# One more chunk in seven block products, its weight forms made earlier, and key transfers issued from GpSimd: a two-layer attention and feed-forward kernel on one Trainium2 core

## The chip, the core and the metric

The kernel runs on one core of one Trainium2 chip. The metric is the device time of one execution in microseconds (us). A core has five engines with an instruction queue each, worked off in the order in which the program lists it: PE (TensorE, matmul), DVE (VectorE), ACT (ScalarE), POOL (GpSimd) and SP (SyncE, which here only issues DMA transfers). ACT and POOL issue DMA transfers too. An engine whose next instruction waits for something holds up all that stands behind it in its own queue.

## The reference

x is 2048 tokens by 576 features, in float32. Two layers with the same weights run one after the other; a layer is an attention part and a feed-forward part.

```python
x = x + _A_ref(_layernorm(x), wqkv, wo)   # 32 heads of 18; token i sees i, i-2, i-4, ..., i-14
x = x + _B_ref(_layernorm(x), w1, w2)     # silu(x @ w1) @ w2, 576 -> 4608 -> 576
x = x + _A_ref(_layernorm(x), wqkv, wo)
x = x + _B_ref(_layernorm(x), w1, w2)
```

## The kernel before, in words

The tokens are cut into four chunks of 512, so two layers make eight stages, s = 0 to 7 (s = 0 to 3 are the first layer's chunks, 4 to 7 the second's). Stage s has a front (`front(s)`, L1208: layer norm, attention, output projection, second layer norm) and a feed-forward part. While PE works on the feed-forward part of stage s, DVE and ACT work on the front of stage s + 1. Float32 products are made of float16 halves: a matmul row is split into a high and a low half, and the products high by high, high by low and low by high are summed.

**The feed-forward part in its plain form** (`ffn`, L1110) is used for s = 0 to 3. For each of 36 blocks of 128 hidden features PE runs 14 matmuls of 128x512 (L1137), ACT applies silu and makes the high half, DVE makes the low half (L1144). After each group of nine blocks the second product follows: 216 matmuls of 128x288 (L1156), whose sums DVE adds to x (`add_to`, L823).

**The form with seven block products** (`ffn_pairs`, L1022) is used for s = 4 to 7. A pair of hidden blocks, the two halves of the 576 input features and the two halves of the chunk make a two by two block product, which is computed with seven products for eight. Each of the seven takes 7 matmuls of 128x256 (L1041), so a pair takes 49. ACT copies a product out of PSUM and applies silu (L1045, L1064 to L1068), DVE adds products up (L1048), and both make the halves of the result (L1071, L1074). The second product is that of the plain form (L1095). This form needs two things that the plain one does not:

- seven combinations of the weights of each of 18 pairs. `prepare(q)` (L927) makes them once: POOL loads the raw weights (L936, L939), DVE forms sums (L947), ACT and DVE make high and low halves (L955, L962) in one buffer `wg`, and POOL stores them to DRAM as `wfs` (L967). Later SP loads them for each stage (L972).
- seven combinations of the normalised tokens. `forms` (L979) takes the place of `layer_norm` there: DVE makes differences (L993, L998), ACT and DVE make the halves (L1007, L1012, L1013), and SP transposes them into `xb` (L1017).

**The attention of one chunk** (`attention`, L677) runs over four units of 144 features. In the first layer the units of s = 1 to 3 are fetched from DRAM (`kv<-kd`, L689). In the second layer PE computes them (L646, 4 tasks of 14 matmuls for each unit), ACT copies them out of PSUM into `kv` and `qt` (L713, L715), and four DMA transfers inside SBUF, `kv<-kv`, bring each partition the keys and values of the partitions ahead of it (`halo`, L720 to L726; these are the key transfers of this text). In the second layer's first block of tokens POOL then saves an edge to DRAM (L734). DVE multiplies, reduces and weighs (L744 to L785), with an exponential on ACT (L767). `project` (L792) splits the result into halves (L803, L421), SP transposes it and PE multiplies by `wo` (L816).

**Order.** The program calls `op(engine, duration, function, reads, writes, priority)` for each piece of work, and `Plan.order` (L111) then lists all pieces for each engine by a list scheduler: an engine takes, of its pieces that are ready by the planner's own durations, the one with the lowest priority number. Front work of stage s has priority s - 1.0, the DVE, ACT and SP work of its feed-forward part s - 0.5, its PE work s + 0.5. `PREP` is the priority of all 18 `prepare` calls; at 2.6 they come behind the front of stage 3 (2.0) and the DVE and ACT work of its feed-forward part (2.5), and ahead of the front of stage 4 (3.0). The layer norm of stage 4 waits for the last `wfs`. The order so made is fixed when the program is built.

Transfers issued from ACT and SP share eight completion counters (`DMAHW0` to `DMAHW7` in the built program), those from POOL have eight of their own (`DMASW0` to `DMASW7`). The counters are given out in the order of the whole program, and an issue waits until the transfer that had its counter before has landed.

Of the kernel before, what the change touches and what calls it, by code (L numbers as in the profile page):

```python
# [16 lines left out]
P = 128  # L17
# [7 lines left out]
NC = 4  # L25
# [3 lines left out]
UC = D // NU  # L29
# [11 lines left out]
LNX = 512.0  # L41
G2 = (5, 4, 5, 4)
W2N = 11
PREP = 2.6


class Buf:
# [204 lines left out]
def sliding_attention_silu_ffn(ctx: ExitStack, tc: tile.TileContext, x, wqkv, wo, w1, w2, out):  # L252
    nc = tc.nc
# [5 lines left out]
    op = S.op  # L259

    def fl(t):
        return t.rearrange("p a b -> p (a b)")
# [5 lines left out]
    def T(b):  # L268
        return S.tags[b.tag][b.slot]
# [91 lines left out]
    def rows(t, row, dims):  # L361
        return bass.AP(tensor=t.tensor, offset=t.offset + row * t.shape[-1], ap=dims)
# [280 lines left out]
    def qkv_matmul(xT, w, j, m):  # L643
        pl = list(passes(lambda k: T(xT)[:, k, j * P:(j + 1) * P], w))
        for n, (a, b) in enumerate(pl):
            nc.tensor.matmul(T(m)[:, :3 * UC], a, b, start=n == 0, stop=n == len(pl) - 1)  # L646
# [30 lines left out]
    def attention(s, xT, wq, more=None):  # L677
        lay, c = divmod(s, NC)
        blk, par = divmod(c, 2)
        pr_ = s - 1.0  # L680
        o = Buf("o")
        for u in range(NU):
            kv, qt = Buf("kv"), Buf("qt")
            own = [(kv, j) for j in range(NJ)]
            if wq is None:
                def fetch(kv=kv, qt=qt, u=u):
                    row = blk * TB
                    q = nc.sync if s == 1 else nc.gpsimd
                    q.dma_start(T(kv).rearrange("p a b c -> p (a b c)"),  # L689
                                rows(kd[par][u], row, [[NJ * 2 * UC, P], [1, NI * 2 * UC]]))  # L690
                    q.dma_start(fl(T(qt)), rows(qd[par][u], row, [[NJ * UC, P], [1, NJ * UC]]))
                op("SP" if s == 1 else "POOL", 1.2, fetch, [("qd", c, u), ("qd0", u) if blk == 0 else ("eds", lay, par, u)],
                   own + [(qt, j) for j in range(NJ)] + [(kv, "halo"), (kv, "edge")], pr_, nbytes=P * 4 * UC * 26)
            else:
                w = wq(u)
                if blk == 0:
                    def clear(kv=kv):
                        nc.gpsimd.memset(T(kv)[0:2, 0:3], 0.0)
                        nc.gpsimd.memset(T(kv)[0:1, 3:7], 0.0)
                    op("POOL", 1.6, clear, [], [(kv, "edge")], pr_)  # L700
                else:
                    def edge(kv=kv, u=u):
                        a, b = T(kv)[0:2, 0:3], T(kv)[0:1, 3:7]
                        e = eds[lay, par, u]
                        nc.sync.dma_start(a.rearrange("p a b c -> p (a b c)"), e[:, 2 * UC:])
                        nc.sync.dma_start(b.rearrange("p a b c -> p (a b c)"), e[1:2, :])
                    op("SP", 0.8, edge, [("eds", lay, par, u)], [(kv, "edge")], pr_, nbytes=20000)
                for j in range(NJ):
                    m = Buf("zq" if lay else "misc")

                    def evac(j=j, m=m, u=u, kv=kv, qt=qt):
                        d = du[:, u:u + 1]
                        nc.scalar.activation(T(kv)[:, j + W - 1].rearrange("p a b -> p (a b)"), T(m)[:, UC:3 * UC],  # L713
                                             AF.Copy, scale=d)
                        nc.scalar.activation(T(qt)[:, j, :], T(m)[:, 0:UC], AF.Copy, scale=d)  # L715
                    op("PE", 2.7 if s else 2.9, lambda j=j, m=m, w=w: qkv_matmul(xT, w, j, m),
                       [(xT, j)] + w.keys, [m, (kv, "hold")] if lay else [m], pr_)
                    op("ACT", 0.9, evac, [m, ("su", u)], [(kv, j), (qt, j)], pr_ - (0 if s else 9))

                def halo(kv=kv):  # L720
                    t = T(kv)

                    for p0, n, i, m in ((0, 112, 3, 4), (112, 15, 3, 4), (0, 112, 0, 3), (112, 14, 0, 3)):
                        d = 1 if i else 2
                        nc.scalar.dma_start(t[p0 + d:p0 + d + n, i:i + m], t[p0:p0 + n, 11 - m:11])
                op("ACT", 3.2, halo, own, [(kv, "halo")], pr_ - 0.2, nbytes=P * 14 * UC * 4)  # L726
                if blk == 0:
                    def save(kv=kv, u=u):
                        t = T(kv)[P - 2:P, 7:11]
                        if lay == 0:  # L730
                            nc.gpsimd.dma_start(rows(kd[par][u], W - 1 + TB - 8, [[NJ * 2 * UC, 2], [1, NJ * 2 * UC]]),
                                                t.rearrange("p a b c -> p (a b c)"))
                        else:
                            nc.gpsimd.dma_start(eds[lay, par, u], t.rearrange("p a b c -> p (a b c)"))  # L734
                    op("POOL", 0.6, save, own, [("eds", lay, par, u)], pr_, nbytes=20000)
                if more:
                    more(u, w)
# [468 lines left out]
    X, XT, ahead = {}, {}, []  # L1206

    def front(s):  # L1208
        X[s] = load_x(s, s - 1.0 if s else -20)
        if s == 0:  # L1210
            no_keys()
            xT = layer_norm(X[0], -20, "xa", 3, PE_LN[0])
            x1 = layer_norm(load_x(1, -8.5, gate[0:1]), -8.5, "xb", False, PE_LN[1])
            x2 = layer_norm(load_x(2, -2.0, gate[3:4]), -2.0, "xb", True, PE_LN[2])

            def more(u, w):
                qkv_ahead(1, u, x1, w)
                qkv_ahead(2, u, x2, w)
                ahead.append((u, w))
            o = attention(0, xT, raw_wq, more)  # L1220
            x3 = layer_norm(load_x(3, -1.2, gate[11:12]), -1.2, "xa", True, PE_LN[3])
            for u in (2, 0, 1, 3):
                store_wq(u, ahead[u][1], PACE_WQ[u])
            for u in (0, 1, 3, 2):
                qkv_ahead(3, u, x3, ahead[u][1] if u != 2 else load_wq(2, -0.95))
            raw_wo()
        elif s < NC:
            o = attention(s, None, None)
        else:
            o = attention(s, layer_norm(X[s], s - 1.0, "xa", False, late=[("wfs", NP - 1)]), lambda u: load_wq(u, s - 1.0, "wz"))  # L1230
        project(s, o, X[s])
        XT[s] = layer_norm(X[s], s - 1.0, "xb", s == 1, s == 0) if s < NC else forms(X[s], s - 1.0)

    front(0)
    for s in range(NL * NC):

        (ffn if s < NC else ffn_pairs)(s, XT[s], X[s])
        if s == 0:
            for q in range(NP):
                prepare(q, PREP)  # L1240
        if s + 1 < NL * NC:
            front(s + 1)
# [29 lines left out]
```

## Time and profile before

| | us |
|---|---|
| median of 3 runs (lowest, highest) | 2207.78 (2200.92, 2210.1) |
| the profiled execution | 2208.64 |
| its span, first to last instruction | 2206.6 |
| busy: PE, DVE, ACT, POOL | 2139.0, 1578.4, 905.3, 347.2 |

The profiled execution lies 0.9 us above the median, and 2.0 us of it lie around the span. Times below are those of the span, counted from its start. The profile is read from the engine that is busy almost all the time (PE) to the few places where it is not, and from there to what it waited for. PE's work falls into clear stages: the feed-forward parts of s = 1 to 7 begin at 482.9, 711.3, 939.6, 1208.8, 1473.8, 1733.3 and 1999.9 us.

### The profile page before, as it was taken

The page shows a single profiled execution, that of the slowest core. Times are in us where ns is not written, and L with a number is a line of the kernel's source. Part 1 is how long each engine was busy: PE and PEld are TensorE (multiplying, and loading weights), DVE is VectorE, ACT ScalarE, POOL GpSimd, SP SyncE. Part 2 cuts the span into 40 slices and gives each one's busy share as a digit, 9 for nine tenths or more (in the row PEclk, how much of TensorE's full clock was granted, in tenths as well). Part 3 has the DMA queues.
Part 4 walks back from the last instruction along what each step waited for, and adds up shares of the span by engine and source line. Part 5 has one row for each costly group of instructions (what it writes and reads, how often), then busy time and mean ns, then how long its engine had stood idle before and what let it go on. Part 6 is the DMA issues. An engine that isn't in the chain of part 4 may idle for free.

```text
span 2206.6 us, 39058 instructions
## 1 busy us (share of the span) xinstructions
PE 2139.0 (97%) x15406; PEld 1503.4 (68%) x15406; DVE 1578.4 (72%) x2453; ACT 905.3 (41%) x1617; POOL 347.2 (16%) x575
## 2 busy tenths in 40 slices
PE   5999999899999999999999989999999998999999
PEld 3556556556666666665667767887788866888887
DVE  7999889799999854454985479755897567963222
ACT  6455676553223333333232333253442424433232
POOL 2133455333012424410000000000000000000000
PEclk9999999999999999999999999999999999999999
DMA  5577576786656576667445765486665954566443
GB/s 154 167 206 254 191 235 221 193 269 221 180 169 224 180 200 214 215 227 194 140 137 125 203 204 172 123 222 158 205 181 151 241 165 128 169 159 192 141 145 107
DMA packets 301776, 407.20 MB, mean 185 GB/s; under 512 B 135432, under 2 KB 220276, under 8 KB 295320
## 3 DMA queue, kind: packets, MB, share of 16 engines
q1 hardware_dynamic: 261936, 270.35, 43.3%
q0 software_dynamic: 31360, 112.83, 15.6%
q10 hardware_dynamic: 8296, 21.52, 3.6%
q8 instruction: 120, 1.97, 0.4%
q14 instruction: 64, 0.52, 0.1%
HBM read 289.62 MB, written 67.68 MB: 162 GB/s over the span
## 4 chain that ended last, share of the span: by engine, by line
PE 90%; DMA 5%; DVE 2%; ACT 1%; issue 1%; ACTq 0%; POOL 0%; SPq 0%; DVEq 0%; POOLq 0%
PE acc L1095 19%; PE acc L1156 19%; PE z L1137 18%; PE misc L1041 8%; PE z L1041 8%; PE z L646 7%; PE misc L646 6%; PE acc L816 5%; DMA kv<-kv 1%; DMA yo<-yh 1%; DMA h<-in_A_wqkv_dram 1%; DMA w1s<-w 1%; DMA w<-in_B_w_dram 1%; DVE pr L777 0%; DMA wq<-wqs 0%
## 5 line engine op out<-in xcount | busy, mean ns | idle before, releaser
L1137 PE MATMUL z<-xb,w 128*128 128x512 f16 x2016 | 443.9, 380 | 12.4 <-ACT hs L1139 5.2
L1095 PE MATMUL acc<-w,h 128*128 128x288 f16 x3456 | 439.2, 286 | 0.6 <-DVE x L1104 0.6
L1156 PE MATMUL acc<-w,h 128*128 128x288 f16 x3456 | 428.6, 286 | 0.0
L1156 PEld LDWEIGHTS <-h 128*128 128x128 f16 x3456 | 338.0, 98 | 88.3
L1095 PEld LDWEIGHTS <-h 128*128 128x128 f16 x3456 | 338.0, 98 | 85.4 <-issue 0.8
L1041 PEld LDWEIGHTS <-w 128*128 128x128 f16 x3528 | 346.3, 98 | 62.6 <-issue 17.3
L1137 PEld LDWEIGHTS <-w 128*128 128x128 f16 x2016 | 197.0, 98 | 247.6 <-DVE w L892 8.2
L823 DVE SCALAR_TENSOR_TENSOR x<-acc,d,x 128x576 f32<-128x576 f32 x135 | 109.8, 814 | 202.7 <-PE acc L1095 131.3
L1041 PE MATMUL misc<-xb,w 128*128 128x256 f16 x1764 | 224.5, 274 | 8.5 <-ACT hs L1064 5.6
L1041 PE MATMUL z<-xb,w 128*128 128x256 f16 x1764 | 224.6, 274 | 7.5 <-ACT hs L1045 7.2
L1139 ACT ACTIVATE hs<-z,d 128x512 f32<-128x512 f32 x144 | 98.4, 683 | 298.1 <-PE z L1137 292.7
L646 PEld LDWEIGHTS <-xa 128*128 128x128 f16 x1344 | 131.7, 98 | 116.8 <-issue 5.2
L744 DVE TENSOR_TENSOR pr<-qt,kv 128x2304 f32<-128x2304 f32 x64 | 163.4, 2554 | 14.3 <-DMA kv<-kv 10.4
L1144 DVE SCALAR_TENSOR_TENSOR h<-hs,sh,h 128x512 f16<-128x512 f32 x144 | 106.3, 747 | 90.0 <-ACT h L1141 89.8
L777 DVE TENSOR_TENSOR pr<-kv,pe 128x1152 f32<-128x1152 f32 x128 | 169.8, 1352 | 1.0
L748 DVE TENSOR_REDUCE lg<-pr 128x128 f32<-128x2304 f32 x64 | 163.1, 2549 | 1.3
L784 DVE TENSOR_TENSOR pr<-pr 128x1152 f32<-128x1152 f32 (+1 forms) x128 | 135.2, 1056 | 3.4
L816 PE MATMUL acc<-wo,yo 128*128 128x288 f16 x896 | 117.1, 291 | 8.0 <-DMA yo<-yh 7.8
L646 PE MATMUL misc<-wq,xa 128*128 128x432 f16 x574 | 112.5, 352 | 3.4 <-ACT xa L436 2.5
L646 PE MATMUL z<-wq,xa 128*128 128x432 f16 x602 | 114.4, 346 | 1.1 <-ACT hs L659 0.6
L816 PEld LDWEIGHTS <-yo 128*128 128x128 f16 x896 | 88.7, 99 | 33.6 <-DMA yo<-yh 8.1
L1180 POOL DMA_DIRECT2D out_dram<-x x12 | 6.5, 544 | 647.9 <-DVE x L823 637.2
(186 smaller groups left out, 2226.8 us busy)
## 6 DMA issues: line engine op xcount, KB each, us to landing
w<-wfs SPq DMA_DIRECT2D x504, 160.0 KB, 3.2
w<-w2s SPq DMA_DIRECT2D x252, 288.0 KB, 4.7
w<-w1s SPq DMA_DIRECT2D x108, 320.0 KB, 4.8
wfs<-xa POOLq DMA_DIRECT2D x18, 1120.0 KB, 5.3
wq<-wqs SPq DMA_DIRECT2D x17, 1080.0 KB, 6.3
kv<-kd POOLq DMA_DIRECT2D x8, 1584.0 KB, 8.0
w1s<-w POOLq DMA_DIRECT2D x36, 320.0 KB, 4.4
w<-in_B_w_dram POOLq DMA_DIRECT2D x36, 288.0 KB, 4.2
```

The source lines that it names most:

```text
L646: nc.tensor.matmul(T(m)[:, :3 * UC], a, b, start=n == 0, stop=n == len(pl) - 1)
L744: nc.vector.tensor_tensor(T(pr), T(qt)[:, j:j + 2, None, :].to_broadcast([P, 2, W, UC]), win(T(kv), j, 2), op=ALU.mult)
L748: nc.vector.tensor_reduce(T(lg)[:, j:j + 2].rearrange("p a w h -> p (a w h)"), T(pr).rearrange("p a w (h d) -> p (a w h) d", d=DH), axis=A ...
L777: nc.vector.tensor_tensor(T(pr)[:, a].rearrange("p w (h d) -> p w h d", d=DH), v, T(pe)[:, j + a, :, :, None].to_broadcast([P, W, UH, DH]) ...
L784: nc.vector.tensor_tensor(t[:, :, 0:h, :], t[:, :, 0:h, :], t[:, :, h:2 * h, :], op=ALU.add)
L816: nc.tensor.matmul(T(acc)[:, h, 0:288], a, b[:, h * 288:(h + 1) * 288], start=n == 0, stop=n == len(pl) - 1)
L823: nc.vector.scalar_tensor_tensor(t, T(acc)[:, :, 0:288], d, t, op0=ALU.mult, op1=ALU.add)
L1041: nc.tensor.matmul(t, w[:, u, :], v[:, r, :], start=first and m == 0, stop=m == 6, skip_group_check=True)
L1095: nc.tensor.matmul(T(acc)[:, h, 0:288], T(hb[t])[:, a, f, j * P:(j + 1) * P], T(wbs[t][f])[:, w, h * 288:(h + 1) * 288], start=t == 0 and ...
L1137: nc.tensor.matmul(T(z), v, u, start=m == 0, stop=m == len(pl) - 1)
L1144: op("DVE", 0.75, lambda hs=hs, h=h, f=f: nc.vector.scalar_tensor_tensor(T(h)[:, 1, :], T(hs), shs[i][:, f:f + 1], T(h)[:, 0, :], op0=ALU. ...
L1156: nc.tensor.matmul(T(acc)[:, h, 0:288], T(hb[q])[:, a, j * P:(j + 1) * P], T(wbs[q][0])[:, w, h * 288:(h + 1) * 288], start=q == 0 and m = ...
```

## The change

A new constant `S2 = 3` stands where the number of chunks, 4, stood in two places: stage 3, the first layer's fourth chunk, now goes through `forms` and `ffn_pairs` in place of `layer_norm` and `ffn`. `PREP` goes from 2.6 to 1.6, so the 18 `prepare` calls come ahead of stage 3's front (2.0). In the second layer (`lay` is 1) the four key transfers of each unit are issued from POOL in place of ACT, and the planner counts 2.6 us of POOL for them in place of 3.2 us of ACT.

```diff
-PREP = 2.6
+PREP = 1.6
+S2 = 3
...
-                        nc.scalar.dma_start(t[p0 + d:p0 + d + n, i:i + m], t[p0:p0 + n, 11 - m:11])
-                op("ACT", 3.2, halo, own, [(kv, "halo")], pr_ - 0.2, nbytes=P * 14 * UC * 4)
+                        (nc.gpsimd if lay else nc.scalar).dma_start(t[p0 + d:p0 + d + n, i:i + m], t[p0:p0 + n, 11 - m:11])
+                op(*(("POOL", 2.6) if lay else ("ACT", 3.2)), halo, own, [(kv, "halo")], pr_ - 0.2, nbytes=P * 14 * UC * 4)
...
-        XT[s] = layer_norm(X[s], s - 1.0, "xb", s == 1, s == 0) if s < NC else forms(X[s], s - 1.0)
+        XT[s] = layer_norm(X[s], s - 1.0, "xb", s == 1, s == 0) if s < S2 else forms(X[s], s - 1.0)
...
-        (ffn if s < NC else ffn_pairs)(s, XT[s], X[s])
+        (ffn if s < S2 else ffn_pairs)(s, XT[s], X[s])
```

The new line moves every later line of the file down by one: L1041 of the kernel before is L1042 of the change.

The two orders are the same on every engine up to the front of stage 3. **First place: DVE, where they part.** DVE is at the projection of stage 2 (L803, L421) and the first multiplication of stage 3's attention (L744). Before:

```order
L803 TENSOR_SCALAR yh<-o,so 128x576
L421 SCALAR_TENSOR_TENSOR yh<-o,so,yh 128x512
L421 SCALAR_TENSOR_TENSOR yh<-o,so,yh 128x64
L744 TENSOR_TENSOR pr_89<-qt_84,kv_82 128x2304
L748 TENSOR_REDUCE lg_86<-pr_89 128x128
L823 SCALAR_TENSOR_TENSOR x_81<-acc_106,d_270,x_81 128x576
```

And of the change (`wq` and `xa` are where the raw and the prepared weights lie):

```order
L804 TENSOR_SCALAR yh<-o,so 128x576
L422 SCALAR_TENSOR_TENSOR yh<-o,so,yh 128x512
L422 SCALAR_TENSOR_TENSOR yh<-o,so,yh 128x64
L963 SCALAR_TENSOR_TENSOR xa<-wq,accw,xa 128x4x256
L963 SCALAR_TENSOR_TENSOR xa<-wq,accw,xa 128x4x128
L963 SCALAR_TENSOR_TENSOR xa<-wq,accw,xa 128x3x256
L963 SCALAR_TENSOR_TENSOR xa<-wq,accw,xa 128x3x128
L745 TENSOR_TENSOR pr_89<-qt_84,kv_82 128x2304
L824 SCALAR_TENSOR_TENSOR x_81<-acc_106,d_270,x_81 128x576
```

Four rows of `prepare` now stand ahead of the multiplication, and so it goes on: up to the projection of stage 3, twelve `prepare` calls have had their sums (L947) on DVE where before six had. On PE that projection moves with them: it stood behind the first 90 of the 216 matmuls of the second product of stage 2's first group, and stands behind the first 18 of the second group's.

PE has the same work ahead of stage 3's feed-forward part in both orders (its row 11298 is the first of that part in both); behind that row it has 36 x 14 matmuls of 128x512 (L1137) before and 18 x 49 of 128x256 (L1042) in the change.

**Second place: ACT, at the third unit of the attention of s = 7**, worked on during the feed-forward part of stage 6 (L713 and L715 copy out keys and queries, L1045 to L1066 belong to the feed-forward part). Before:

```order
L713 ACTIVATE kv_82<-misc_104,du 128x288
L715 ACTIVATE qt_84<-misc_104,du 128x144
L1045 ACTIVATE wq<-misc_103 128x256
L725 DMA kv_82<-kv_82 112x1152
L725 DMA kv_82<-kv_82 15x1152
L725 DMA kv_82<-kv_82 112x864
L725 DMA kv_82<-kv_82 14x864
L1045 ACTIVATE hs<-z_101 128x256
L1064 ACT_TABLE_LOAD
```

And of the change:

```order
L714 ACTIVATE kv_82<-misc_103,du 128x288
L716 ACTIVATE qt_84<-misc_103,du 128x144
L768 ACTIVATE pe_88<-lg_86 128x256
L1046 ACTIVATE wq<-z_101 128x256
L1046 ACTIVATE wq<-z_102 128x256 x2
L1046 ACTIVATE hs<-misc_103 128x256
```

The four issues are gone from between the copies. On POOL they stand between the write of stage 5's result and that of stage 6's (`out_dram`), where before these writes followed one another. **Third place: POOL, from the last write of stage 5's result on.** Before:

```order
L1180 DMA out_dram<-x_81 128x576
L1180 DMA out_dram<-x_74 128x576
L1180 DMA out_dram<-x_75 128x576
L1180 DMA out_dram<-x_76 128x576
L1180 DMA out_dram<-x_77 128x576
```

And of the change, the first two of the four units that stand between the two results:

```order
L1181 DMA out_dram<-x_81 128x576
L726 DMA kv_82<-kv_82 112x1152
L726 DMA kv_82<-kv_82 15x1152
L726 DMA kv_82<-kv_82 112x864
L726 DMA kv_82<-kv_82 14x864
L726 DMA kv_83<-kv_83 112x1152
```

Each unit's four transfers follow the one before's; no other kind of work stands between them there.

## The prediction

> **What bounds the kernel now.** I read the page first: busy times, slices, and the shares of the chain that ended last.
>
> ```profile
> PE 2139.0 (97%) x15406; PEld 1503.4 (68%) x15406; DVE 1578.4 (72%) x2453; ACT 905.3 (41%) x1617; POOL 347.2 (16%) x575
> PE   5999999899999999999999989999999998999999
> DVE  7999889799999854454985479755897567963222
> PE 90%; DMA 5%; DVE 2%; ACT 1%; issue 1%; ACTq 0%; POOL 0%; SPq 0%; DVEq 0%; POOLq 0%
> ```
>
> PE is the bound: past the first slice it is busy 90% or more, but for three slices with an 8. DVE is nearly full through 14 slices (to 772 us) and has room behind them. So a term counts if it shortens PE's work, ends a PE wait, or makes PE wait.
>
> Next, the stages: PE's windows from stage 1 on, one for each feed-forward part (length, then the busy time of PE, PEld, DVE, ACT, POOL, with counts).
>
> ```profile
> 482.90:711.20 228.30, 228.30 (x1482) 144.65 (x1480) 221.01 (x261) 80.77 (x106) 40.78 (x69) 1.00 0.65 205
> 711.20:939.60 228.40, 228.40 (x1482) 144.78 (x1481) 137.65 (x217) 83.70 (x115) 89.16 (x149) 1.00 0.67 208
> 939.60:1208.80 269.20, 269.20 (x1706) 166.66 (x1704) 185.05 (x273) 87.68 (x150) 20.54 (x31) 1.00 0.56 161
> 1208.80:1473.70 264.90, 259.03 (x2084) 204.31 (x2082) 186.59 (x291) 99.92 (x202) 8.02 (x12) 0.99 0.64 181
> 1473.70:1733.30 259.60, 256.93 (x2084) 203.56 (x2083) 185.70 (x289) 98.41 (x198) 2.16 (x4) 1.00 0.66 181
> 1733.30:1999.80 266.50, 259.05 (x2084) 204.14 (x2082) 183.18 (x280) 98.74 (x198) 2.16 (x4) 0.99 0.63 171
> ```
>
> In stages 1 to 3 PE never pauses. Stages 4 to 6 do the same work three times in 264.9, 259.6 and 266.5 us; what differs is idle time.
>
> **The change part by part.** *The products of stage 3.* The chain of waits, in order of time, has the unit costs (start, length, what):
>
> ```profile
> 738.62 11.03 PE acc L1156 x90
> 749.65 3.43 PE acc L816 x28
> 778.80 27.20 PE z L1137 x126
> 913.30 26.46 PE acc L1156 x216
> 1208.98 3.06 PE z L1041 x28
> 1295.33 2.56 PE misc L646 x14
> ```
>
> A plain stage has 36 x 14 = 504 matmuls of 128x512, 4 x 27.20 = 108.8 us. The seven-product form has 18 x 49 = 882 at 3.06 / 28 = 0.109 us, 96.4 us. The rest is common to both: 4 x 26.46 = 105.8 for the second product, 16 x 2.56 = 41.0 for keys, queries and values, 4 x 3.43 = 13.7 for the projection, 160.5 together. The plain stage comes out at 269.3, where the window shows 269.2, so such sums hold. The new stage 3 is 96.4 + 160.5 = 256.9: **-12.3 us**, if nothing stops PE.
>
> *The key transfers.* By the same sum stages 4 to 6 should take 3 x 256.9 = 770.7 us; the windows add up to 791.0. So 20.3 us are lost. The groups of 1209 to 2000 us show where (last figure: idle time ahead, and what ended it):
>
> ```profile
> L1041 PE MATMUL misc<-xb,w 128*128 128x256 f16 x1339 | 170.5, 275 | 8.5 <-ACT hs L1064 5.6 <-ACT wq L1045 2.7
> L1041 PE MATMUL z<-xb,w 128*128 128x256 f16 x1309 | 167.5, 274 | 7.5 <-ACT hs L1045 7.2
> ```
>
> 16.0 us of idle, in three stalls of 5.6, 2.7 and 7.2, each ended by ACT freeing a PSUM bank. The timeline shows what held ACT there:
>
> ```profile
> 1306.12 9.77 ACTq L725 DMA_DIRECT2D kv<-kv  x4
> 1315.93 0.47 ACT L1064 ACTIVATE hs<-misc,accw 128x256 f32<-128x256 f32 x1 [9.57 <-DMA kv<-kv]
> 1316.46 1.65 PE L1041 MATMUL misc<-xb,w 128*128 128x256 f16 x7 [5.61 <-ACT hs L1064]
> ...
> 1569.69 6.91 ACTq L725 DMA_DIRECT2D kv<-kv  x4
> 1577.08 0.93 PE L1041 MATMUL misc<-xb,w 128*128 128x256 f16 x7 [2.67 <-ACT wq L1045]
> ...
> 1824.38 10.55 ACTq L725 DMA_DIRECT2D kv<-kv  x4
> 1834.98 0.38 ACT L1045 ACTIVATE hs<-z 128x256 f32<-128x256 f32 x1 [10.28 <-DMA kv<-kv]
> 1835.41 1.65 PE L1041 MATMUL z<-xb,w 128*128 128x256 f16 x7 [7.18 <-ACT hs L1045]
> ```
>
> Each time it is the third unit's four transfers. The fourth issue waits for a completion counter whose last transfer is still under way (the third unit's own in stages 4 and 6, the weights `wq` in stage 5), and PSUM copies stand behind it. All transfers of this kind from 1200 us on:
>
> ```profile
> L725 ACTq DMA_DIRECT2D kv<-kv x48: 534/816/1148, 1261.8 to 1873.5; - x48
> DMA to landing us min/median/max: 6.9/8.1/9.3
> ```
>
> An issue itself takes 0.5 to 1.1 us; the 7 to 10 us are waits for a landing. On POOL none of it stands ahead of a PSUM copy, and POOL's own eight counters are never back at the first while a unit's four are given out. So the mechanism goes, in stage 3 too, where PE now uses the narrower products. Of the 20.3 I take all 16.0 of idle and half of the 4.3 by which the matmuls after the stalls are slow: **-18 us**; ends 0 and -20.3.
>
> What the transfers cost on POOL the trace shows only by its neighbours, the fetches of stages 1 to 3:
>
> ```profile
> L689 POOL DMA_DIRECT2D kv<-kd x8: 528/542/566, 347.0 to 667.6; - x8
> DMA to landing us min/median/max: 6.3/7.9/10.2
> ```
>
> A larger transfer issued from POOL takes 0.53 to 0.57 us to issue and 7.9 to land, against 8.1 for those on ACT. So keys arrive between 2 us sooner and 3 us later (6.3 - 8.1, 10.2 - 6.9); I take no change. It concerns DVE alone, which is idle 70 us and more in each of stages 4 to 6, and POOL, busy 2 to 8 us there. The Trainium skill speaks against this edit: in "SBUF — State Buffer", section "Summary: rules for kernel authors", it advises against a transfer issued from POOL beside DVE work, since DVE in a two-port mode keeps POOL from writing descriptors. The rows just quoted lie where DVE is 97% busy (its 221.01 of 228.30) and show no issue above 0.57 us, so the trace does not bear it out. A second page, "DMA: Bandwidth & Descriptors", section "Issuing engines are not separate DMA queues", says that another issuing engine only saves the time of issuing, "usually small"; by it this term would be near 0, and the 9.77 us row speaks against that too.
>
> *The weight forms ahead of stage 3's attention.* This adds no work, but it moves DVE work into its fullest stretch. Cost and places:
>
> ```profile
> L962 DVE SCALAR_TENSOR_TENSOR xa<-wq,accw,xa 128x1024 f16<-128x1024 f32 (+1 forms) x72 | 62.0, 912 | 3.0 <-ACT xa L955 3.0
> L947 DVE TENSOR_TENSOR wq<-wq 128x384 f32<-128x384 f32 x72 | 36.9, 554 | 0.9
> 586.15 2.55 DVE L744 TENSOR_TENSOR pr<-qt,kv 128x2304 f32<-128x2304 f32 x1
> 740.89 0.52 DVE L803 TENSOR_SCALAR yh<-o,so 128x576 f16<-128x576 f32 x1
> 784.37 3.40 DVE L962 SCALAR_TENSOR_TENSOR xa<-wq,accw,xa 128x1024 f16<-128x1024 f32 x4 [0.29 <-ACT xa L955]
> 981.82 3.41 DVE L962 SCALAR_TENSOR_TENSOR xa<-wq,accw,xa 128x1024 f16<-128x1024 f32 x4 [0.78 <-ACT xa L955]
> ```
>
> One call costs DVE (62.0 + 36.9) / 18 = 5.5 us. Six more stand ahead of the projection of stage 3: 33 us, at 97% busy 34, so DVE splits that result at 740.9 + 34 = 775, not 740.9. In the new order PE comes to it behind the rest of the first group and the whole first product of the second: the second product from 738.6 without the projection, 26.46, to 765.1, then 27.20, then 18 matmuls, 2.2, so at 794.5 where it was 749.65. Before, the lead was 749.65 - 740.9 = 8.8 us; now it is 19.5. So: **0**. The cover is gone if the calls themselves are slow. They follow one another through one buffer: making, storing, landing. Where nothing else filled DVE, ten such cycles ran from 784.37 to 981.82 (first and last of eleven splits), 19.7 us each. Nine calls' splits stand between 586 us, where the orders part, and the projection; eight cycles make 158 us, and there are 189. It would break above 189 / 8 = 23.6 us a cycle.
>
> *The token forms of stage 3* replace a layer norm. Their price before, for stage 4:
>
> ```profile
> 1185.10 1.07 DVE L993 TENSOR_SCALAR xa<-x,mv,nt 128x576 f32<-128x576 f32 x2
> 1213.02 2.54 SPq L1017 DMA_TRANSPOSE xb<-yh  x2
> ```
>
> The last differences stood 24 us ahead of the products (1208.98), the last transposes 4 us behind them, and PE did not wait. In the change DVE has the last differences behind its work on the last block of stage 2's first product, and PE leaves that block one second product, 26.46 us, ahead of stage 3: about the same lead. **0**; ends 0 and, if all of it came late, the 28 us from 1185.1 to 1213.0.
>
> **The sum.** 2208.64 - 12.3 - 18 = **2178 us** for the profiled execution; the median of the runs shown is 0.9 us lower, which I leave out.
>
> **The rivals.** *Only the products pay* (the waits move to another engine or another unit, or stage 3 gets a stall of its own). For it: in the change ACT has an exponential (L768) where the transfers stood, which waits for DVE; against it: of the 12 units of stages 4 to 6, nine had no stall with the same neighbours. Time: 2208.6 - 12.3 = 2196; with a stall in stage 3 like the average of the others (20.3 / 3 = 6.8), 2203.
>
> *Keys come late from POOL.* This is what the skill's rule would do. If each of a unit's four issues lasted as long as a DVE multiplication, 2.55 us and not 0.54, the keys would be 8 us late; only the first unit of a stage has no cover, so 4 x 8 = 32 us of DVE lateness, against 70 us of room in a stage. It gives 2178 to 2210. The L689 row speaks against it.
>
> *The weight forms hold up stage 3* (the other side). If a cycle takes 30 us, half as long again as that mean, DVE comes to the projection 8 x (30 - 23.6) = 51 us after 775. Of the lead of 19.5 us, 8.8 was enough before, so 10.7 is spare; PE waits 51 - 10.7 = 40 us, and the time is 2218; at 33 us a cycle it is 2242. It decides from 23.6 + 10.7 / 8 = 25 us a cycle. For it: POOL's queue now has key fetches of stage 3 (L689) among these loads and stores; against it: the mean of 19.7.
>
> *The change does not do what it says*: excluded by the order, which shows 882 matmuls of 128x256 in stage 3 and no key transfers on ACT in the second layer.
>
> **How the numbers follow.** Forecast 0.62 (2171 to 2187: half of the 20.3 recovered is 2186, all of it 2176, and one of the three runs before lies 7 us below their median). Only the products 0.21 (2188 to 2203). Late keys 0.07 (2180 to 2210). Weight forms 0.10 (2205 to 2242). The range 2171 to 2200 holds the first, most of the second and half of the third, somewhat over 8 in 10. Two kernels closer than 0.5%, 11 us, cannot be told apart here; against 2207.8 that bound is 2196.7. Faster: 0.62, 0.11 of the second, 0.04 of the third, 0.77. Same: 0.10, 0.03 and 0.02 of the last, 0.15. Slower: 0.08.
>
> **What would show it.** Products: the window of stage 3 is 257 us from an unchanged start at 939.6, its first product about 96 us by the chain. Key transfers: no idle above 1 us ahead of L1042, and windows of 257 in stages 4 to 6. Weight forms: no idle ahead of L817 in stage 2 and 18 stores finished by about 910. Token forms: no idle ahead of the first L1042. It is wrong if PE waits at the projection in stage 2, or if stalls of 5 us stay in stages 3 to 6 with ACT or DVE as their end.

## The result and the profile after

| | before | after |
|---|---|---|
| median (lowest, highest), us | 2207.65 (2200.92, 2210.1) | 2189.35 (2184.02, 2198.78) |
| profiled execution, us | 2208.64 | 2198.78 |
| from the begin of stage 1 to the end of the span, us | 1723.7 | 1705.3 |

The ratio is 0.9918, with an interval from 0.9891 to 0.9945: the change makes the kernel faster, by about 18 us, where 30 were forecast. The profiled execution is the slowest of the four of the change. It comes to stage 1 at 491.7 us, 8.8 later than that of before, although the instructions up to there and on to 586 us stand in the same order; such begins lie between 480.5 and 491.7 in the runs below. So traces are compared from the begin of stage 1 on (last row of the table): -18.4 us, which agrees with the medians. The forecast in the same measure is 1723.7 - 30.3 = 1693.4.

The page of the change, PE's slices and the shares of the chain:

```profile
PE 2132.9 (97%) x15784; PEld 1541.9 (70%) x15784; DVE 1598.0 (73%) x2513; ACT 927.2 (42%) x1697; POOL 380.9 (17%) x639
PE   5999999899999999999999999999999999999999
PE 87%; DMA 6%; DVE 4%; ACT 1%; issue 1%; POOL 0%; SPq 0%; ACTq 0%; DVEq 0%; POOLq 0%
```

Of PE's three slices with an 8 only the one in the head is left; the shares of the chain that fell to DMA and DVE have grown. The windows of stages 1 to 6:

```profile
491.70:720.50 228.80, 228.54 (x1483) 144.76 (x1481) 218.88 (x273) 86.56 (x115) 69.12 (x118) 1.00 0.73 229
720.50:948.80 228.30, 228.30 (x1482) 144.87 (x1480) 157.55 (x247) 93.02 (x142) 70.02 (x116) 1.00 0.68 211
948.80:1207.70 258.90, 257.25 (x2084) 203.58 (x2082) 184.91 (x287) 99.70 (x202) 20.22 (x32) 1.00 0.67 184
1207.70:1466.30 258.60, 257.57 (x2084) 203.63 (x2082) 188.06 (x297) 98.48 (x198) 16.45 (x28) 1.00 0.68 184
1466.30:1731.30 265.00, 260.17 (x2091) 205.00 (x2090) 185.99 (x286) 97.06 (x197) 10.70 (x20) 0.99 0.67 181
1731.30:1991.10 259.80, 257.69 (x2085) 203.59 (x2084) 183.13 (x280) 95.95 (x196) 10.70 (x20) 1.00 0.63 174
```

Stage 3 went from 269.2 to 258.9. Stages 4 to 6 went from 791.0 to 783.4, where 773 was forecast. What is left there is seen in the groups of 1206 to 1990 us:

```profile
L1042 PE MATMUL misc<-xb,w 128*128 128x256 f16 x1351 | 170.8, 274 | 3.4 <-DVE wq L1049 2.2 <-DMA w<-wfs 1.1
L1042 PE MATMUL z<-xb,w 128*128 128x256 f16 x1302 | 165.0, 273 | 4.4 <-DMA w<-wfs 3.3 <-DVE h L1075 0.6 <-DVE wq L1049 0.5
L745 DVE TENSOR_TENSOR pr<-qt,kv 128x2304 f32<-128x2304 f32 x24 | 61.3, 2555 | 18.1 <-DMA kv<-kv 17.5
```

No idle ends with ACT. PE now waits for weights to land (`w<-wfs`, 4.4 us) and for DVE, and DVE stands 17.5 us for keys, in three waits, each at the first unit of a stage; before it was 9.0 us in two. All key transfers of 1200 to 2000 us, issued and landed:

```profile
L726 POOL DMA_DIRECT2D kv<-kv x48: 515/541/563, 1258.1 to 1844.6; - x48
...
DMA to landing us min/median/max: 4.3/8.4/11.0
```

An issue takes 0.54 us in the middle, and they land in 8.4. The largest of PE's waits is again at the third unit, of stage 5. The timeline there:

```profile
1553.86 0.32 SPq L593 DMA_DIRECT2D wq<-wqs  x1
...
1554.59 1.05 SPq L834 DMA_DIRECT2D w<-w2s  x2
1554.66 2.11 POOL L726 DMA_DIRECT2D kv<-kv  x4 [24.28 <-ACT qt L716]
...
1556.09 15.41 SPq L973 DMA_DIRECT2D w<-wfs  x15
...
1567.25 0.94 PE L1042 MATMUL z<-xb,w 128*128 128x256 f16 x7 [2.75 <-DMA w<-wfs]
```

And the windows of 5 us around it (last three columns: granted clock, DMA share, GB/s):

```profile
1545.00:1550.00 5.00, 5.00 (x29) 2.65 (x28) 4.90 (x4) 1.54 (x4) 0.00 (x0) 1.00 0.44 149
1550.00:1555.00 5.00, 5.00 (x32) 3.03 (x31) 4.93 (x3) 1.54 (x4) 0.34 (x1) 1.00 0.13 17
1555.00:1560.00 5.00, 5.00 (x48) 4.47 (x46) 4.75 (x8) 1.65 (x5) 1.76 (x4) 1.00 0.86 286
1560.00:1565.00 5.00, 4.49 (x41) 3.74 (x39) 4.93 (x7) 3.94 (x7) 0.00 (x0) 1.00 1.05 267
1565.00:1570.00 5.00, 2.75 (x17) 2.12 (x18) 3.47 (x7) 2.18 (x5) 0.00 (x0) 0.81 1.06 324
```

The DMA engines are nearly idle, then full: the unit's weights (1080 KB) and the keys (997 KB) are issued within 3 us, fifteen loads of block weights (160 KB each) from 1556.09 to 1571.5, and PE runs out of block weights. In the window in which the wait ends the granted clock is 0.81, and of the matmuls behind it the next fourteen took 3.14 us, where fourteen take 1.69 a little later: a wait costs more than its own length.

### The profile page after: what moved, and what is told of

Read it like the earlier page. It is cut to its first block, busy times and chain, and to the rows that moved or that the text cites. A ratio compares the mean times of both kernels' runs of the same rounds, so it can differ in the third digit from the quotient of the medians.

```text
span 2197.0 us, 40182 instructions
## 1 busy us (share of the span) xinstructions
PE 2132.9 (97%) x15784; PEld 1541.9 (70%) x15784; DVE 1598.0 (73%) x2513; ACT 927.2 (42%) x1697; POOL 380.9 (17%) x639
## 4 chain that ended last, share of the span: by engine, by line
PE 87%; DMA 6%; DVE 4%; ACT 1%; issue 1%; POOL 0%; SPq 0%; ACTq 0%; DVEq 0%; POOLq 0%
PE acc L1096 24%; PE acc L1157 13%; PE z L1138 13%; PE z L1042 10%; PE misc L1042 10%; PE z L647 7%; PE misc L647 5%; PE acc L817 5%; DMA w<-wfs 2%; DMA yo<-yh 1%; DMA w<-in_B_w_dram 1%; DVE pr L778 1%; DMA h<-in_A_wqkv_dram 1%; DVE pr L785 1%; DVE yh L422 0%
## 5 line engine op out<-in xcount | busy, mean ns | idle before, releaser
L1042 PEld LDWEIGHTS <-w 128*128 128x128 f16 x4410 | 431.8, 98 | 67.9 <-DMA w<-wfs 8.2
L1138 PE MATMUL z<-xb,w 128*128 128x512 f16 x1512 | 336.9, 383 | 11.5 <-ACT hs L1140 4.2
L1042 PE MATMUL misc<-xb,w 128*128 128x256 f16 x2226 | 280.3, 273 | 3.9 <-DVE wq L1049 2.2
L1138 PEld LDWEIGHTS <-w 128*128 128x128 f16 x1512 | 148.8, 99 | 191.0 <-DVE w L893 7.5
L1042 PE MATMUL z<-xb,w 128*128 128x256 f16 x2184 | 276.2, 273 | 5.6 <-DMA w<-wfs 4.0
L745 DVE TENSOR_TENSOR pr<-qt,kv 128x2304 f32<-128x2304 f32 x64 | 163.4, 2553 | 20.7 <-DMA kv<-kv 19.5
L1140 ACT ACTIVATE hs<-z,d 128x512 f32<-128x512 f32 x108 | 73.7, 682 | 165.8 <-PE z L1138 162.3
L1075 DVE SCALAR_TENSOR_TENSOR h<-wq,sh,h 128x1024 f16<-128x1024 f32 x60 | 76.8, 1280 | 65.0 <-ACT h L1072 65.0
L1145 DVE SCALAR_TENSOR_TENSOR h<-hs,sh,h 128x512 f16<-128x512 f32 x108 | 79.5, 746 | 34.7 <-ACT h L1142 34.4
```

What stands on the lines that cost most here:

```text
L745: nc.vector.tensor_tensor(T(pr), T(qt)[:, j:j + 2, None, :].to_broadcast([P, 2, W, UC]), win(T(kv), j, 2), op=ALU.mult)
L1042: nc.tensor.matmul(t, w[:, u, :], v[:, r, :], start=first and m == 0, stop=m == 6, skip_group_check=True)
L1138: nc.tensor.matmul(T(z), v, u, start=m == 0, stop=m == len(pl) - 1)
L1145: op("DVE", 0.75, lambda hs=hs, h=h, f=f: nc.vector.scalar_tensor_tensor(T(h)[:, 1, :], T(hs), shs[i][:, f:f + 1], T(h)[:, 0, :], op0=ALU. ...
```

## The experiments

Two theories for the part of the 18 us forecast for the key transfers that was not got. **Theory DMA:** the third unit's burst fills the DMA engines, and PE waits for weights behind the keys' bytes. **Theory keys:** DVE's waits for the keys set back the work that empties PSUM for PE. All times are from the begin of stage 1 (b) as well as medians; before is 1723.7 by b. There is one trace of each kernel, so b has the spread of a single execution: the two traces of the change differ by 3.3 us (1705.3 and 1702.0).

| run | median, us | ratio to before (interval) | b, us |
|---|---|---|---|
| e1 the change again | 2189.8 | 0.9926 (0.9903 to 0.9948) | 1702.0 |
| e2 keys from POOL alone | 2204.13 | 0.9977 (0.9961 to 0.9992) | 1719.6 |
| e3 all but the keys | 2205.22 | 0.9981 (0.9961 to 1.0001) | 1713.7 |
| e4 early weight forms alone | 2219.31 | 1.0056 (1.0034 to 1.0077) | 1739.5 |
| e5 no key transfers | 2173.99 | 0.9859 (0.9829 to 0.9888) | 1692.7 |
| e6 later landing planned | 2190.43 | 0.992 (0.99 to 0.9939) | 1704.2 |
| e7 keys from SP | 2193.86 | 0.9939 (0.9917 to 0.9961) | 1708.5 |
| e8 two transfers a unit | 2188.49 | 0.991 (0.9891 to 0.993) | 1702.0 |
| e9 thin keys | 2177.09 | 0.9836 (0.9823 to 0.9848) | 1695.3 |
| e10 unit weights from POOL | 2197.86 | 0.9932 (0.9915 to 0.9949) | 1714.9 |
| e11 e10 and e8 together | 2202.26 | 0.9951 (0.9939 to 0.9963) | 1716.3 |
| e12 keys unread | 2176.56 | 0.9854 (0.9825 to 0.9883) | 1695.3 |

**e1, the change as it is.**

> The changed kernel once more, for its spread and a second trace. In its first trace PE lost 14.5 us in stages 3 to 6 (258.7, 258.7, 265.0, 259.7 us where the sum gives 256.9), in a 4.6 us wait for weights in stage 5 and some ten of 0.3 to 1.6 us; and stage 1 began at 491.7, 9 us later than in the kernel before, although the order is the same up to 586 us. If the 9 us are chance, stage 1 begins nearer to 483 now and the time is 2184 to 2190. If they belong to the change, the start stays at 490 or above. If the 4.6 us wait belongs to the order, it is in this trace too, at the third unit of stage 5.

The change repeats, and the late begin of stage 1 does not (486.2). Stages 3 to 6 took 259.2, 258.3, 261.8 and 260.2 us. Stages 4 to 6 add up to 780.3, 10.7 less than before. The longest wait for weights is at the third unit of stage 5 again, 2.3 us for 2.75 in the first trace (not the 4.6 that the expectation names), so it belongs to the order.

**e2, the key transfers from POOL alone.** `S2` and `PREP` as before (4 and 2.6).

> Only the key transfers go from POOL; stage 3 in its plain form, weight forms late. The prediction's term: -18 us, 2190, and no PE idle above 1 us ahead of L1041. If the traces of the two kernels add up (20.3 us lost in stages 4 to 6 before, 12.7 after): -7.6 us, 2200, with waits for weights and for DVE in place of those for ACT. If the change lives from its products alone: 2207.

It gained 4.1 us by b, 0.23% by the ratio. The groups of 1206 to 2000 us, where before had 16.0 us of idle ended by ACT:

```profile
L1041 PE MATMUL misc<-xb,w 128*128 128x256 f16 x1351 | 171.5, 273 | 6.4 <-DMA w<-wfs 4.6 <-DVE wq L1048 1.8
L1041 PE MATMUL z<-xb,w 128*128 128x256 f16 x1302 | 165.5, 273 | 6.2 <-DMA w<-wfs 2.8 <-ACT wq L1045 1.7 <-DVE wq L1048 1.6
```

The stalls behind ACT's issues went (1.7 us that end with ACT are left), and 7.4 us of waiting for weights came in their place. Stages 4 to 6 took 787.8 us for 791.0.

**e3, everything but the key transfers.** They stay on ACT:

```diff
-(nc.gpsimd if lay else nc.scalar).dma_start(
+nc.scalar.dma_start(
-op(*(("POOL", 2.6) if lay else ("ACT", 3.2)), halo,
+op("ACT", 3.2, halo,
```

> Seven products for stage 3 and the early weight forms, key transfers left on ACT. The products save 12.3 us. In this order the fourth transfer of the third unit has its own unit's counter again in stages 3 and 6, so if the counters make the stalls, there is one of 5 to 8 us in each of them (ACT held by kv<-kv) and none of that size from the unit's own counter elsewhere: 2195 to 2203. If the stalls came from something else and the products are all there is: 2189, as the whole change.

The products alone gained little, because a stall came to stage 3 that it had not had. The timeline of the third unit of stage 3:

```profile
1050.34 0.47 ACT L1065 ACTIVATE hs<-misc,accw 128x256 f32<-128x256 f32 x1 [10.47 <-DMA kv<-kv]
...
1050.86 1.65 PE L1042 MATMUL misc<-xb,w 128*128 128x256 f16 x7 [6.51 <-ACT hs L1065]
```

Stage 3 took 264.8 us for 258.9 in the change. With the transfers on POOL this stall is absent, so the products pay in full only with the other edit. The stalls came where the counters put them: 6.5 us in stage 3 and 6.4 in stage 6, and at most 2.65 in stages 4 and 5. That supports the account of completion counters. The gain is 10.0 us by b but 3.0 by the medians, with an interval that reaches 1, and the time lies above the 2195 to 2203 that were expected.

**e4, the early weight forms alone.** `PREP = 1.6`, nothing else.

> Only the priority of the weight forms, 1.6 for 2.6: stage 3 plain, keys on ACT. The prediction costs it at nothing: no PE idle at the projection of stage 2, stages 1 to 3 at 228, 228 and 269 us, time 2203 to 2209 (stalls of 5 to 8 us move with the counters). If the early forms hold DVE up, PE waits ahead of L816 in stage 2 and the time is above 2212.

It was slower, by 15.8 us as measured by b and 11.1 by the medians. Stage 2 took 235.4 us for 228.4. The timeline of 838 to 862 us:

```profile
838.08 0.57 POOL L967 DMA_DIRECT2D wfs<-xa  x1 [0.17 <-issue]
...
854.62 1.76 ACT L955 ACTIVATE xa<-wq,accw 128x1024 f16<-128x1024 f32 x2 [7.49 <-DMA wfs<-xa]
...
857.00 5.23 PE L1137 MATMUL z<-xb,w 128*128 128x512 f16 x16 [5.31 <-ACT hs L1139]
```

And two windows of the same stretch:

```profile
840.00:845.00 5.00, 5.00 (x25) 2.23 (x23) 1.50 (x2) 2.46 (x4) 0.00 (x0) 1.00 1.19 117
845.00:850.00 5.00, 5.00 (x25) 2.25 (x23) 0.75 (x1) 1.41 (x2) 0.00 (x0) 1.00 1.20 81
```

One store of weight forms took 16.4 us to land, where the median is 5.5; the DMA engines were full (1.19, 1.20) with little moved (117 and 81 GB/s): of the 2711 packets from 838 to 850 us 2414 were under 512 bytes, and the last two transposes of stage 3's normalised tokens (`xb<-yh`, L438) had been issued from 834 to 841 us. ACT needs the buffer that the store reads, stood at L955, and the silu that PE waited for was behind it in ACT's queue. The rest of the loss lies in the third-unit stalls of stages 4 to 6, with 21.2 us of idle at the products for 16.0 before. In the change the slowest such store landed in 10.0 us and PE did not pause in stage 2.

**e5, no key transfers in the second layer.**

```diff
-op(*(("POOL", 2.6) if lay else ("ACT", 3.2)), halo, own, ...
+if lay == 0:
+    op("ACT", 3.2, halo, own, ...
```

> The change without the key transfers of the second layer: keys and values of the partitions ahead are left as they stand in the buffer. It tells what the transfers still cost. Theory DMA: at the third unit the 16 DMA engines are full (share 0.95 to 1.06 for 12 us in the two traces of the change), and PE waits for weights because bytes are short; without these 1.0 MB the wait of 2.5 to 4.6 us in stage 5 goes. Theory keys: the small waits ended by DVE (some 0.7 us each, 3 to 4 us in all) come from DVE standing 19.5 us for keys; they go. With both: losses in stages 3 to 6 from 11.8 to 2 to 4 us, 2181. If the weights are late for a reason of SP's own, the wait stays and the time is 2186 to 2190.

The data that the transfers bring is left out here. Stages 3 to 6 took 258.4, 256.8, 258.0 and 257.0 us: the sum of the prediction, 256.9, is nearly reached. So what the change leaves hangs on the keys in some way: their bytes, their landing, or the order that the planner makes around them, which is another one here.

**e6, the planner counts 31 rows for 14 as the transfers' bytes,** so that it plans their landing later, as the trace has it.

> The change with the planner told that the keys land later: 2.2 us of POOL and 31 rows of bytes for 14, so 11.2 us from issue to landing in its reckoning, where it had 7.8 and the trace has 8.5 at the median and 11.0 at most. Nothing else is edited; the order is made anew. Theory keys: DVE is no longer sent to a unit whose keys are not there, its waits fall from 19.5 us to under 5 and the small PE waits go, -3 us, 2186 to 2187. Theory DMA: the wait for weights stays, 2187 to 2190.

DVE's wait for keys fell from 17.5 to 13.8 us, PE's for weights rose from 4.4 to 5.9, and the time did not move.

**e7, the key transfers from SP** (`nc.sync`, 2.0 us of SP planned).

> The change with the key transfers issued from SP. It separates being away from ACT from being on POOL. If only ACT's release counts: 2189, as the change. If waits for completion counters count wherever they stand: the fourth transfer now holds SP, and the weights behind it come late, PE idle ended by w<-wfs of 5 us and more at the third units: 2195 to 2205.

PE's waits for weights were 6.0 us; the transfers took up to 2.5 us each in SP's queue, ahead of the loads of weights. 6.5 us longer than e1 by b, 4.1 by the medians: between the two cases that were expected.

**e8, two transfers a unit** of 127 and 126 partitions in place of four of 112, 15, 112 and 14.

> The change with two key transfers for each unit in place of four: 127 and 126 partitions in one each, the same bytes, POOL counted at 1.3 us. POOL's issue shrinks from 2.1 to 1.1 us, so keys could land 1 us sooner, 7 to 8 us, and DVE's wait of 19.5 shrink by 4 to 5: 2187 to 2190. If a transfer over 127 partitions runs on few DMA engines, keys land far later (20 us and more), DVE waits at each stage's first unit and PE behind it: above 2200.

No difference that can be told: landing in 8.9 us (median) for 8.4, DVE's wait 17.2 for 17.5.

**e9, thin keys.**

```diff
-dma_start(t[p0 + d:p0 + d + n, i:i + m], t[p0:p0 + n, 11 - m:11])
+dma_start(t[p0 + d:p0 + d + n, i, 0, :], t[p0:p0 + n, 11 - m, 0, :])
```

> The change with the same order, the same four key transfers of each second-layer unit from POOL and the same waits for them, but each carries one token's keys of 144 features, 576 bytes of a partition, in place of three or four tokens' keys and values, 3456 or 4608 bytes. The other keys and values of the partitions ahead stay as they stand, so part of the data is left out. It parts the wait for the keys from their bytes, which the run without key transfers took away together (2173.99 us). Theory DMA (the bytes fill the DMA engines at the third unit, and PE waits for the weights wfs behind them): the idle of PE that ends at w<-wfs goes to under 1 us in each of stages 4 to 6, and the time is 2173 to 2181. Theory keys (the small DVE waits for the keys are what is left): landing is a latency of 4 us and more whatever the bytes, so DVE's idle at the first multiplication of the attention falls from 17.5 only to some 8 to 12 us, and the time is 2183 to 2189.

The order is that of the change, row by row on every engine. Not only the bytes differ, though: a thin transfer reads one token, so it needn't wait until all four tasks of the unit have been copied out. At the third unit of stage 5 the keys went at 1532.93 and 1535.48, ahead of `wq` at 1539.80; in the change they went at 1554.66, behind `wq`:

```profile
1532.93 1.06 POOL L727 DMA_DIRECT2D kv<-kv  x2 [22.78 <-ACT qt L716]
1535.48 1.06 POOL L727 DMA_DIRECT2D kv<-kv  x2 [1.50 <-ACT kv L714]
```

The groups of 1206 to 1990 us (L1045 is L1042 here, L748 is L745), and the landing of the transfers:

```profile
L1045 PE MATMUL misc<-xb,w 128*128 128x256 f16 x1382 | 173.1, 273 | 1.6 <-DVE wq L1052 1.2 <-DMA w<-wfs 0.3
L1045 PE MATMUL z<-xb,w 128*128 128x256 f16 x1344 | 169.9, 273 | 0.8 <-DMA w<-wfs 0.8
L748 DVE TENSOR_TENSOR pr<-qt,kv 128x2304 f32<-128x2304 f32 x24 | 61.3, 2553 | 0.6
```

```profile
DMA to landing us min/median/max: 1.6/1.9/4.1
```

What theory keys expected of the landing (4 us and more whatever the bytes) is wrong: it fell to 1.9. DVE's wait went too, by the shorter landing and the earlier issue together. PE's wait for weights went at the same place of the program, the third unit of stage 5, where SP lets the same burst go without the keys' bytes:

```profile
1536.50:1541.50 5.00, 5.00 (x34) 3.23 (x33) 3.86 (x3) 1.55 (x4) 0.04 (x1) 1.00 0.20 40
1541.50:1546.50 5.00, 5.00 (x48) 4.49 (x46) 4.30 (x8) 1.88 (x5) 0.00 (x0) 1.00 0.98 386
```

What the DMA queues moved in the 13.8 us from `wq` on, in the change (1553.5 to 1567.3; `q1` has SP's transfers, `q0` POOL's) and in e9 (1539.5 to 1553.3), in packets, MB and share of the sixteen engines:

```profile
q1 hardware_dynamic: 1113, 2.48, 64.5%
q0 software_dynamic: 272, 1.02, 26.3%
```

```profile
q1 hardware_dynamic: 2336, 3.87, 82.5%
```

So with the keys' 1.02 MB in the burst SP's weights come at 2.48 MB, without them at 3.87. In this order, then, the keys in the burst cost: stages 4 to 6 took 774.8 us for 780.3 in e1 and 783.4 in the change's profile. PE's idle at the products fell from 7.8 to 2.4 us: 3.3 of it were waits for weights and 2.1 waits for DVE, so each theory has a part.

**e10, the unit weights from POOL.** `load_wq` of the second layer issues `wq<-wqs` from POOL in place of SP, whose queue had stood 90.0 us at it.

> The change with the second layer's loads of the key and query weights (wq<-wqs, 1.1 MB a unit) issued from POOL in place of SP. Nothing is left out. In the trace of the change SP stood at these issues for 90.0 us in 10 waits for PE, longest 11.2 us, with the loads of wfs queued behind them: at the third unit of stage 5 the DMA engines were 0.44 and 0.13 busy in the ten microseconds before SP was let go, and 0.86 to 1.06 in the fifteen behind. Theory DMA, put more narrowly: the burst is made by SP's queue, which holds back weights that could have been loaded ahead; with the wait on POOL they are loaded in the gap, and PE's idle that ends at w<-wfs falls from 4.4 us to under 1.5; time 2178 to 2185. Theory DMA as first put (the bytes alone fill the engines): the idle stays at 3 to 5 us and the time at 2187 to 2192. Theory keys: the keys now stand behind a 1.1 MB load on POOL's queues and land 2 to 4 us later, time 2192 to 2200.

Not what was hoped for: 12.9 us longer than e1 by b, and about the same by the ratio. What SP waits for, and the windows of the same stretch:

```profile
SPq L834 <- PE acc L1096: 206.6, 76, 34.4
```

```profile
1550.00:1555.00 5.00, 5.00 (x36) 3.33 (x35) 4.93 (x3) 1.55 (x4) 1.76 (x4) 1.00 0.17 26
1555.00:1560.00 5.00, 4.34 (x40) 3.68 (x38) 4.86 (x9) 1.73 (x5) 0.93 (x2) 1.00 0.87 287
```

The planner put loads of the second product's weights (L834) where `wq` had been, and SP stood at those, 206.6 us for 112.6. The gap and the burst remained, and the thought behind this run was mistaken. There are twelve buffers for block weights (`wf`) and one for the second layer's `wq` (`wz`), and up to 1550 us, ahead of the burst, the loads and the products of the change stood so:

```profile
L973 SPq DMA_DIRECT2D w<-wfs x299: 319/320/2077, 907.2 to 1511.0; - x150
L1042 PE MATMUL z<-xb,w x1015: 270/273/283, 948.8 to 1510.7; 128*128 128x256 f16 x170
L1042 PE MATMUL misc<-xb,w x994: 269/273/283, 951.9 to 1495.3; 128*128 128x256 f16 x199
```

The 2009 matmuls are 287 products of seven, so twelve loads lay ahead, and every buffer was full: in the change SP held back no block weights at `wq`, and the gap could not be filled with them from any queue. In e10 the counts up to 1552 us are the same.

**e11, e10 with two transfers a unit.**

> The run before with the key transfers of a unit as two of 127 and 126 partitions in place of four. Nothing is left out. Two transfers for four took the time from 2189.8 to 2188.5 in the change, no difference that can be told. Theory DMA: the same here, within 3 us of the run before, 2177 to 2185. Theory keys: two issues less, 1.1 us a unit, so keys land earlier and the time is 3 to 5 us below the run before.

The same as e10 within 1.4 us by b, 4.4 us slower by the medians. Fewer issues do not help here either.

**e12, the keys at full size, written to a spare place in DRAM.**

```diff
-dma_start(t[p0 + d:p0 + d + n, i:i + m], ...), halo, own, [(kv, "halo")]
+dma_start((kx if lay else t)[p0 + d:p0 + d + n, i:i + m], ...), halo, own, [("kx",) if lay else (kv, "halo")]
```

> The change with the second layer's key transfers at full size, four a unit from POOL, but written to a spare place in DRAM, for which nobody waits; the keys and values of the partitions ahead stay as they stand, so that part of the data is left out. Thin transfers gave 2177.09 us and a landing of 1.9 us for 8.4, so both the bytes and the wait went together there; here the bytes stay and DVE's wait goes (the way of the bytes differs: to DRAM and not inside SBUF). If the load is what is left of the cost (Theory DMA), PE's idle that ends at w<-wfs stays at 3 us or more in stages 4 to 6 and the time is 2184 to 2191. If DVE's wait for the keys is (Theory keys), the time is that of no transfers, 2173 to 2179, with under 1.5 us of idle at w<-wfs. In between, 2179 to 2184: both have a part.

Theory DMA as first put does not hold in this order: the bytes are there, and PE's idle at the products is 0.1 us. The groups of 1206 to 1990 us, the windows around the third unit of stage 5, and SP's and POOL's part of the timeline:

```profile
L1042 PE MATMUL z<-xb,w 128*128 128x256 f16 x1374 | 173.4, 273 | 0.1
L1042 PE MATMUL misc<-xb,w 128*128 128x256 f16 x1372 | 172.3, 273 | 0.0
```

```profile
1565.00:1570.00 5.00, 5.00 (x49) 4.47 (x47) 2.39 (x5) 4.29 (x8) 0.98 (x2) 1.00 0.95 314
1570.00:1575.00 5.00, 5.00 (x47) 4.33 (x45) 4.71 (x8) 4.87 (x9) 0.00 (x0) 1.00 1.04 385
```

```profile
1547.14 4.08 SPq L973 DMA_DIRECT2D w<-wfs  x6
...
1552.89 5.40 SPq L973 DMA_DIRECT2D w<-wfs  x5
...
1563.08 0.32 SPq L593 DMA_DIRECT2D wq<-wqs  x1
...
1563.85 11.17 SPq L973 DMA_DIRECT2D w<-wfs  x12
1563.88 2.10 POOL L726 DMA_DIRECT2D kx<-kv  x4 [25.35 <-ACT qt L716]
```

The burst is as full as in the change (0.95 and 1.04). But eleven loads of block weights stand ahead of `wq` in SP's queue; in the change there were none between the last edge load at 1543.5 and `wq` at 1553.86. A planner that knows of no wait for the keys lays the stage out in another order. Full buffers are not what differs: nearly twelve loads lay ahead here too (310 loads and 2086 matmuls up to 1562.8 us). In the change PE ran the unit's key products in one piece, from 1543.4 to 1553.7 us, used no block weights meanwhile, and then ran twelve block products without a break until it waited. In e12 block products stand between the key products, and behind ten of them PE turns to the second product; two loads of `w2s`, 576 KB, are not in the burst. Which of these, or the keys' way to DRAM, spares PE the wait is not shown.

## Why the prediction was right, and where it was not

**The products of stage 3: right.** Predicted 256.9 us; 258.9 in the change, 259.2 in e1, 257.9 in e9, with 257.25 of PE busy. The gain is 10.3 us for 12.3; 1.6 of the missing 2.0 are small waits, most of them for weights. That nothing stops PE was true only with the other edit: in e3 the products alone brought 4.4 us of stage 3, since ACT's fourth issue stalled there too.

**The key transfers: the step that failed in its size.** The prediction took -18 us of the 20.3 lost in stages 4 to 6. It measured -7.6 in the change's profile and -10.7 in e1. The mechanism was right: all 16.0 us of idle ended by ACT went. But the prediction's own sign, no idle above 1 us ahead of these matmuls, did not come. The step that failed is "So keys arrive between 2 us sooner and 3 us later; I take no change. It concerns DVE alone". The first half held: they landed in 8.4 us (median) for 8.1. The second did not: PE stood 7.8 us at the products of stages 4 to 6, 4.4 for weights and 3.3 for DVE. With thin keys that go earlier (e9) these stages took 774.8 us, and without keys (e5) 771.8, against a predicted 773. So the transfers cost 5.5 to 11.6 us more than was counted, and by a way that the prediction did not look at: the DMA engines, by which PE gets its weights. A stall taken away from ACT left PE to meet the next limit at the same unit.

**The weight forms: right for the change, with less room than was reckoned.** Stage 2 is 228.30 us with PE busy 228.30. The last store was issued at 917.6, 426 us behind the begin of stage 1; 427 was forecast for its end. But the lead at the projection was forecast at 19.5 us and came out at 8.6 (DVE splits at 794.99, PE begins at 803.54): a cycle took 22.2 us (eight between the stores of 608.5 and 786.3) and not 19.7; by the prediction's reckoning PE would wait from 25 on. And e4 shows the rival of this edit at work, by another road than the one priced: ACT and not DVE, at silu and not at the projection, by one slow landing of 16.4 us. Why the change escapes it is only argued: its stage 3 has the transposes of the token forms (L1018) in place of those of L439, at other times.

**The token forms: right.** PE waited 0.4 us for DVE in all of stage 3, and never for the forms.

**The rivals.** "Only the products pay" (2196 to 2203) was too slow for the whole change; it describes e2 and e3, where a wait moves to weights or to another unit. "Keys come late from POOL" was wrong in its mechanism: issues on POOL took 0.54 us in the middle, beside DVE at 185 of 265 us. The rule of the Trainium skill on POOL's issues beside DVE ("SBUF — State Buffer", section "Summary: rules for kernel authors") holds there for DVE's 2x and 4x modes. No row here tells in which mode DVE ran, so these runs show no such delay and do not refute the rule. Of the eight issues that the prediction set beside a DVE 97% busy, five lie in that stage, stage 1; the other three were no slower. The other page of the Trainium skill, "DMA: Bandwidth & Descriptors", section "Issuing engines are not separate DMA queues", says that the engines' transfers share the same sixteen DMA engines; that half of it the burst at 1560 us bears out, with a share of 1.05 in which SP's and POOL's transfers ran together. Its small saving from another issuer, which the prediction set aside, is nearer to e2's 4.1 us than the 18 were, though the stalls on ACT did go.

**What stays open.** Whether the time between e1 and e12 is due to the order that the planner makes when it counts the landing, to DVE's wait in the run itself, or to the other way of the bytes (they landed in 6.7 us in DRAM) wasn't parted. e9 shows that in the change's order fewer bytes, sent ahead of the burst, are enough; which of the two it takes wasn't parted either. By the medians e9 lies 12.7 us below e1 and by b 6.7: some 5 us of it lie ahead of stage 1, where the orders are the same, and are not explained. A kernel that does all the work and is faster than the change wasn't found: e6, e7, e8, e10 and e11 are not. One that spreads the block products of the third unit, as e12 does, and keeps the keys was not tried.

## What to carry to other kernels

When a stall of the bounding engine is taken away, ask which of its inputs would run short next at that place, and read the DMA share and the loading queue in the windows around it: the gap and the burst show side by side. Then count the loads that lie ahead against the buffers that there are, before you blame the queue that stands: here all twelve buffers were full, so an earlier issue had nowhere to put its data, and what helped was less beside the loads (e9) or another order (e5, e12). An edit that frees one engine's queue should be priced with the bytes that it issues and with who else needs the DMA engines then. And the parts of a change are not summed from runs of one part each: by b they brought 4.1 and 10.0 us apart (e2, e3) and 18.4 to 21.7 together, by the medians 4.0 and 3.0 apart and 18.4 together (e1).

## What the runs showed of the hardware

- Behind two transposes by DMA the engines stood at a share of 1.19 to 1.20 with only 81 to 117 GB/s moved, 2414 of 2711 packets being under 512 bytes; a 1120 KB store among them landed in 16.4 us for a median of 5.5 (e4).
- Key transfers of 576 bytes a partition landed in 1.9 us, of 3456 and 4608 bytes in 8.4 us, both four a unit from POOL (e9 and the change); the thin ones also went earlier, so the bytes and what else the engines had to move are not parted.
- Two transfers over 127 and 126 partitions landed in 8.9 us, as four of 112 and 15 or 14 do (e8).
- In the 2.75 us behind a wait of PE of 2.75 us the granted clock was 0.65, and 0.70 in the 2.5 us behind those (the change); behind a wait of 2.29 us in e1 it stayed at 1.00.
